# A new hand-over list for a linear-attention-plus-FFT-convolution kernel: order, engines and PSUM banks

## The chip, the cores and the metric

The kernel runs on one core of one Trainium2 chip. The core has engines that each take their own instructions strictly in the order in which the program gives them: TensorE (PE in the profile; its weight loads are shown apart as PEld), VectorE (DVE), ScalarE (ACT), GpSimd (POOL) and SyncE (SP), which here only issues transfers. They wait for one another through semaphores. PE writes its results to eight PSUM banks; DVE and ACT read them, POOL works on SBUF alone. The metric is device microseconds (us) for one execution; lower is better. A difference under about 2% is called no change.

## What is computed

The input is r, k, v, w of shape 4 x 8 x 768 x 48 (batch, heads, time, head width) and u. First comes a recurrence over time for every batch and head, then, on its output seen as 4 x 768 x 384, a gated convolution through the Fourier transform, and an output product:

```python
for t in range(S):
    cur = np.einsum('bhd,bhe->bhde', u[None] * kt, vt)
    y[:, :, t] = np.einsum('bhd,bhde->bhe', rt, state + cur)
    state = wt[:, :, :, None] * state + np.einsum('bhd,bhe->bhde', kt, vt)
...
proj = x @ w_proj
x1, x2, x3 = (proj[..., :D], proj[..., D:2 * D], proj[..., 2 * D:])
x2_conv = np.fft.irfft(np.fft.rfft(x2, n=S, axis=1) * np.fft.rfft(filter_fft, n=S, axis=0), n=S, axis=1)
return ((x1 * x2_conv * x3) @ w_out)
```

## The kernel before

**The two halves of the work.** The 768 time steps of a batch are cut into three groups of 256, so there are twelve groups, numbered 0 to 11 in the names; a group holds two chunks of 128 rows. For each group the kernel loads w, k, r, v (`lw`, `lk`, `lr`, `lv`), takes the logarithm of w on ACT (`ln`), sums it over time on PE (`cs`, lines 1325 and 1328), takes the exponential on ACT (`ex`, `ph`), multiplies k and r with it on DVE (`km`, `qm`, line 1353, tile kq), turns the result round on PE (`tk`, `tq`, line 1366) and copies it out of PSUM (`ck`, `cq`, tile qk). `sc` (line 1464) are the scores, `mt` their masked copy on DVE, `kv` and `ki` the state's product, `su` its scaling on DVE (tile S), `ys`, `yy` and `yi` (lines 1445, 1486, 1500) the output, `xn` its copy, `yt` and `xT` its turned copy. Beside that run small products on plain SBUF tiles: `rk` = r times k, `kw` and `rw` (k and r times w, tile kr), `vb` (v in bf16), `vc` (v times the bonus of u, which comes by `rp`, `rt`, `cp`, `cc`), and `ws`, a product of two rows of w before the logarithm (tile wp). Where `ws` is left out, `ln` takes both rows and `cs` takes twice as many matmuls.

After every third group a batch is complete and its second half can be done: `p` and `q` (line 1712) are two of the projections and `xw` (line 1736) the third, `f` (line 1564) the forward transform, `u` and `z` the product in the frequency domain, `E` (line 1803) the inverse transform, `cE`, `aE`, `dE`, `yE` its putting together and gating, `o` (line 1884) the output product, `co` its copy and `so`, `to` the stores. `cp` and `cq` with two numbers behind them (`cp0.2.0`, `cq0.0.0`) are the copies and gates of the projections; where an `xq` stands ahead of a `cq`, ACT copies the product out of PSUM first and the gate reads SBUF, otherwise the gate reads PSUM. The inverse transform has two forms: folded (`Q`), whose matmuls are shorter and which needs the four `dE` additions behind it, and whole (`P`), which does not.

**Who sets the order.** Nothing is scheduled by a planner when the program is built. A table of text, `ORDER`, has a line for each of some 900 operations: its name, a letter for the engine or form (P PE, A ACT, D DVE, G POOL, S SP; N and B are second forms of DVE and ACT, `-` leaves the operation out), and the PSUM banks of the results that it opens. The program walks the table from top to bottom and issues each operation on the engine named:

```python
o = self.ops.pop(name)
place["how " + name] = e
for key in o.banks:
    place[key] = int(more.pop(0))
if e == NONE:
    continue
got = o.fns[e](e, place)
...
if more and got is not None and more[0] in last:
    tie(got, last[more[0]])
```

So the table sets three things at once: the order on each engine (and on the queue of transfers of SP), the engine of each operation, and the banks. A name at the end of a line (`kw0 G rw0`) is a tie: this operation also waits for that one of DVE. A line `warm 22 2` issues matmuls of zeros on PE into a bank that is free (here 22 units of 256 columns, as 11 matmuls of 512); they compute nothing. All loads and stores but three are issued by SP; `turn` operations with the letter S are transposing transfers, which then need neither PE nor a copy.

Of the kernel before, what the change touches and what calls it, by code (L numbers as in the profile page):

```python
# [89 lines left out]
ph0 A  # L90
# [2 lines left out]
lv1 S
lk2 S
lx1 -
lr2 S
is A
if0 A
sin1 A
um P 4  # L100
warm 4 6
rp0 P 5
rw0 D
qm0 D
kw0 G rw0
rk1 G
vb0 G
warm 8 7
# [63 lines left out]
cq1 A
table A
sc1.0 P 4
lr4 S
rt2 A
dW2 S
dW0 S
lw4 S
ma0.1 -  # L180
mt0.1 D
yy0 P 2
yi0 P
lk4 S
ma1.0 -
lx3 -
xn0 A
xn1 A
rw3 G
vb3 G  # L190
vb2 G
mt1.0 D
ys2 P 6
ys3 P 4
sc1.1 P 2
warm 4 1
cp2 P 0
ma1.1 -
cc2 A
ln2 B  # L200
mt1.1 D
warm 3 1
rp3 P 1
ki3 P 0
kv3 P
cs2 P 2
rt3 A
ln3 B
su3 D
# [152 lines left out]
xq0.0.0 A
sd0.0.0 D
sd0.1.0 D
xq0.2.1 -
rt6 A
f0.0 P 6
cq0.2.1 D
cq0.0.0 N
cc5 D  # L370
cp6 P 4
ws6 G cq0.0.0
lr7 S
lw7 S
lk7 S
lv6 S
cxw1.0 A
cf0.0 A
cc6 D
ys8 P 0  # L380
ys9 P 2
ln6 A
sc4.1 P 4
ma4.1 -
mt4.1 D
kw6 G
rw6 G
f0.1 P 6
lw8 S
lk8 S  # L390
lr8 S
cf0.1 A
cs6 P 4
lx5 -
# [1601 lines left out]
```

## Time and profile before

| what | us |
|---|---|
| median of 3 runs | 151.16 |
| the runs | 149.73, 151.16, 151.60 |
| span of the profiled execution | 149.4 |

The page gives the span of the profiled execution and no time of its own beside it; the lowest of the three runs is 0.3 us above that span. How to read the page: a share of busy time is a share of the span, so PE's 93% says only that some matmul was in flight, since matmuls overlap. More telling is the busy time of each engine in a stretch, and the chain of work that ended last, which is followed backwards from the last instruction to whatever released each step. "A x12" in a row means twelve instructions of one kind in a row. Line numbers are those of the kernel before; in the changed kernel every line is two lower, as its table is two lines shorter.

### The profile page before, as it was taken

Reading aid. Unit: us, or ns where it says so; the run is one execution under the profiler, and the core shown is the slowest. Engines: PE = TensorE matmul, PEld = TensorE weight load, DVE = VectorE, ACT = ScalarE, POOL = GpSimd, SP = SyncE. Lnnn points to the kernel's source line nnn. Section 1 sums busy time; section 2 is a strip of 40 time slices with the busy share of each in tenths; the row PEclk is TensorE's granted clock in tenths of the full one; section 3 lists DMA queues with packets and bytes.
Section 4 is the critical chain, followed back from the end, with each engine's and each line's share of the span. In section 5 each row is a group of like instructions: output and inputs, shape, how many; then the busy total and the mean of one; then the engine's idle time right before and its main releaser. Section 6 shows DMA issues by size and latency. Waiting matters only on the chain.

```text
span 149.4 us, 5795 instructions
## 1 busy us (share of the span) xinstructions
PE 138.7 (93%) x2441; PEld 91.1 (61%) x2441; DVE 123.6 (83%) x239; ACT 120.2 (80%) x200; POOL 91.8 (61%) x104
## 2 busy tenths in 40 slices
PE   7999999999998999999999799999999999999960
PEld 2456766857676766766767555566766566566510
DVE  6999972994859689889999957999987999999920
ACT  3789979869897978899999578898868677687660
POOL 7959979999997439649929676960675006005100
PEclk9999999999999999999999999999999999999995
DMA  4999989999999989999999837799921420502775
GB/s 111 325 321 312 276 193 323 324 257 276 276 251 227 214 214 307 243 281 215 303 202 314 226 59 125 147 275 153 213 103 31 136 53 0 211 24 88 316 254 167
DMA packets 69596, 31.18 MB, mean 209 GB/s; under 512 B 65217, under 2 KB 67778, under 8 KB 69570
## 3 DMA queue, kind: packets, MB, share of 16 engines
q1 hardware_dynamic: 69408, 30.61, 82.9%
q8 instruction: 19, 0.31, 0.8%
q10 hardware_dynamic: 162, 0.20, 0.6%
q14 instruction: 7, 0.06, 0.1%
HBM read 22.41 MB, written 4.72 MB: 182 GB/s over the span
## 4 chain that ended last, share of the span: by engine, by line
PE 60%; POOL 17%; DVE 9%; DMA 5%; issue 3%; ACT 3%; POOLq 0%; SPq 0%; DVEq 0%
PE banks L1712 15%; PE banks L1564 10%; PE banks L1884 8%; PE banks L1736 6%; PE banks L1803 5%; POOL kr L1126 5%; DMA kr<-in_r_dram 5%; POOL rk L1126 4%; POOL vc L1126 4%; PE banks L1486 3%; PE banks L1425 2%; PE banks L1464 2%; DVE kq L1353 2%; PE banks L1366 2%; ACT X L1130 2%
## 5 line engine op out<-in xcount | busy, mean ns | idle before, releaser
L1126 DVE TENSOR_TENSOR mt<-banks,causal 128x1024 bf16<-128x1024 f32 x21 | 25.6, 1220 | 6.6 <-PE banks L1464 6.5
L1712 PE MATMUL banks<-xT,wproj 128*128 128x384 bf16 x144 | 27.1, 326 | 0.5 <-ACT X L1130 0.3
L1353 DVE TENSOR_TENSOR kq<-banks,kr 128x768 bf16<-128x768 f32 x24 | 22.1, 950 | 2.9 <-ACT banks L1336 1.6
L1126 POOL TENSOR_TENSOR rk<-kr 128x768 bf16<-128x768 f32 x11 | 20.0, 1814 | 6.0 <-DVE U L1126 3.2
L1126 POOL TENSOR_TENSOR kr<-kr,w 128x384 f32<-128x384 f32 x21 | 20.6, 998 | 4.9 <-DVE sd L1748 2.8
L1130 ACT ACTIVATE x<-banks 128x768 bf16<-128x768 f32 (+1 forms) x28 | 19.4, 715 | 4.3 <-PE banks L1712 2.3
L1712 PEld LDWEIGHTS <-wproj 128*128 128x128 bf16 x144 | 13.3, 97 | 9.3 <-issue 0.8
L1126 POOL TENSOR_TENSOR vc<-vb,cc 128x768 bf16<-128x768 bf16 x12 | 17.6, 1474 | 1.1 <-DVE mt L1126 0.8
L1126 POOL TENSOR_TENSOR g<-g,x 128x384 bf16<-128x384 bf16 (+1 forms) x5 | 6.0, 1204 | 15.8 <-DVE g L1126 9.4
L1130 ACT ACTIVATE X<-banks 128x768 bf16<-128x768 f32 x12 | 9.8, 814 | 5.4 <-PE banks L1564 4.2
L1564 PE MATMUL banks<-sd,F 128*128 128x384 bf16 (+1 forms) x96 | 13.6, 327 | 0.4 <-ACT X L1130 0.3
L1736 PE MATMUL banks<-wproj,xT 128*128 128x384 bf16 x72 | 13.3, 326 | 0.2 <-ACT wproj L1130 0.2
L1884 PE MATMUL banks<-wout,y 128*128 128x384 bf16 (+1 forms) x78 | 13.5, 328 | 0.1
L1152 PE MATMUL banks<-wt 128*128 128x512 bf16 (+1 forms) x37 | 12.3, 441 | 1.1 <-DVE wt L1219 1.1
L1564 PEld LDWEIGHTS <-F 128*128 128x128 bf16 (+1 forms) x120 | 9.0, 103 | 5.3 <-issue 1.1
L1126 DVE TENSOR_TENSOR U<-X,hh 128x768 bf16<-128x768 bf16 (+1 forms) x17 | 12.1, 728 | 0.2
L1130 ACT ACTIVATE o<-banks 128x768 f32<-128x768 f32 (+1 forms) x13 | 9.6, 768 | 2.9 <-PE banks L1884 2.6
L1130 ACT ACTIVATE xn<-banks 128x384 bf16<-128x384 f32 x24 | 10.6, 491 | 1.2 <-PE banks L1500 1.1
L1464 PE MATMUL banks<-qk 48*64 48x128 bf16 x384 | 10.1, 219 | 0.7 <-DVE kq L1353 0.6
L1130 ACT ACTIVATE qk<-banks 128x1024 bf16<-128x1024 bf16 x10 | 9.9, 1019 | 1.1 <-PE banks L1366 1.1
L1336 ACT ACTIVATE banks<-banks 128x768 f32<-128x768 f32 x12 | 9.6, 799 | 1.0 <-PE banks L1328 0.9
L1126 POOL TENSOR_TENSOR wp<-w 128x384 f32<-128x384 f32 x7 | 7.0, 1005 | 5.1 <-DMA w<-in_w_dram 2.9
(123 smaller groups left out, 312.1 us busy)
## 6 DMA issues: line engine op xcount, KB each, us to landing
w<-in_w_dram SPq DMA_DIRECT2D x12, 384.0 KB, 6.0
kr<-in_k_dram SPq DMA_DIRECT2D x12, 384.0 KB, 5.5
kr<-in_r_dram SPq DMA_DIRECT2D x12, 384.0 KB, 6.0
v<-in_v_dram SPq DMA_DIRECT2D x12, 384.0 KB, 4.8
out_dram<-o SPq DMA_DIRECT2D x11, 384.0 KB, 2.6
o<-in_moe_w_proj_dram SPq DMA_DIRECT2D x4, 384.0 KB, 6.0
U<-in_moe_filter_fft_dram SPq DMA_DIRECT2D x4, 288.0 KB, 8.2
o<-in_moe_w_out_dram SPq DMA_DIRECT2D x1, 384.0 KB
```

Of the source, the lines that this page charges most:

```text
L1126: return eng(e).tensor_mul(o, a, b)
L1130: return nc.scalar.activation(out=o, in_=a, func=AF.Copy)
L1152: nc.tensor.matmul(banks[:, at, lo:hi], wt[:, 0:L], x, start=True, stop=True)
L1336: return nc.scalar.activation(out=p, in_=p, func=AF.Exp)
L1353: op(f"{t}{gi}", [DVE], lambda e, bk, m=m: nc.vector.tensor_mul(kqq[:, m, :, :, 0:D], _mid(two(bk, f"cs{gi}")[:, 1 - m, 0:C].rearrange("p ...
L1464: nc.tensor.matmul(p[spans[c], par, i, jk, :].rearrange("p (j t) -> p j t", j=2), qkk[x, 0, jk, 2 * a + i, spans[c]], qkk[x, 1, :, 2 * a + ...
L1486: nc.tensor.matmul(yview(bk, c)[:, par, hp, :], mt[sm][spans[c], a, par, q, jk, :], vbb[spans[c], 2 * hp + par, jk, :], start=(pi == 0 and ...
L1564: nc.tensor.matmul(p[rows], F[:, ti, c0 + rows.start:c0 + rows.stop], x[q][:, ti, :], start=(ti == 0), stop=(ti == NT - 1),)
L1712: nc.tensor.matmul(o, wproj[:, cb, col0:col0 + L], x, start=(cb == 0), stop=(cb == CB - 1))
L1736: nc.tensor.matmul(view(bk)[:, z], xT[bx][:, c0 + z, cb], wproj[:, cb, C:2 * C], start=(cb == 0), stop=(cb == CB - 1),)
L1803: nc.tensor.matmul(o, P[:, q, m, cs], x, start=start, stop=stop)
L1884: nc.tensor.matmul(view(bk)[:, j] if full else view(bk)[spans[j]], y[cb][:, j, p0:p0 + m], wout[:, cb, :], start=(cb == 0), stop=(cb == CB ...
```

## The change

Only the table `ORDER` differs; the functions are the same. All 915 operations are in both tables. The new table stands in a new order throughout, with other banks, and 140 operations have another letter. The first lines show the kind of change:

```diff
 wz D
 uo D
+imaps G
+maps G
+smalls D
+lw0 S
+lk0 S
+lr0 S
+lw1 S
...
-rk0 D
-rw0 D
-vb0 G
+rk0 G
+rw0 G
+vb0 D
...
-ws4 G
+ws4 -
-cE0.2 B
+cE0.2 A
-aE0.2.0 D
+aE0.2.0 N
...
```

By kind, the letters that change are these. From POOL to DVE, 26: `vb0`, `vc0`, `vc3`, `vc6`, `vc8`, `vc9`, `rw3`, `rk4`, `kw4`, `kw6`, `rk11`, `ws9`, `ws10`, two casts of weights (`eW3`, `eW4`), `kz0`, four gates (`cq0.2.0`, `cq1.2.1`, `cq2.2.1`, `cq3.0.1`), three `sd3` and three `dE`. From DVE to POOL, 14: `rk0`, `rw0`, `kw7`, `rw7`, `sd0.0.0`, three `u`, three `dE`, three `yE`. From ACT to DVE: `ck1`, `cq1`, `cq2`, `ck5`, `xn4`, `xn6`, `xn7`, `rt5`, `rt6`, `vb6`, `eV1`, `co3.2`; the other way `ck2`, `ck4`, four `cc`, `cxw3.5`. `vb4` goes from POOL to ACT. `ws4`, `ws5`, `ws7` and `ws8` are left out. Twelve of the thirteen `xq` copies of ACT and two of three `ma` (the same for scores) are left out, so the gates and masks behind them read PSUM. Eleven `cE` copy the whole inverse transform with ACT instead of half of it, so that 22 `aE` read SBUF only. `E1.2` and `E2.0` take the whole form, and their four `dE` go. `yt4`, `yt6`, `tq6` and `rp9` become transposing transfers on SP. The fillers are 71 units instead of 69, put elsewhere.

At the program's start ACT's list reads as follows, first before, then now. u_r is u in bf16 (the operation `ur`), lg the logarithm of w.

```order
L1235 DMA u_f_142<-in_u_dram 1x384
L1232 ACT_TABLE_LOAD
L1314 ACTIVATE lg1_72<-w1_62 128x8x2x48
L1130 ACTIVATE u_r_143<-u_f_142 1x768
L1314 ACTIVATE lg0_71<-w0_61 128x8x2x48
L1336 ACTIVATE banks_146<-banks_146 128x2x384 x2
L1339 ACTIVATE phi1_78<-banks_146 128x8
```

```order
L1233 DMA u_f_142<-in_u_dram 1x384
L1230 ACT_TABLE_LOAD
L1128 ACTIVATE u_r_143<-u_f_142 1x768
L1312 ACTIVATE lg0_71<-w0_61 128x8x2x48
L1337 ACTIVATE phi0_77<-banks_146 128x8
L1312 ACTIVATE lg1_72<-w1_62 128x8x2x48
L1334 ACTIVATE banks_146<-banks_146 128x2x384 x2
```

The cast of u now stands ahead of both logarithms, and one exponential's column (phi) ahead of the second logarithm.

PE's list at the same place, first the kernel before, where its 11 fillers end (nothing stands ahead of them) and the first sum over time begins, then the new one, from the product with u_r through the 11 fillers to the first sum:

```order
L1152 LDWEIGHTS wt_140
L1152 MATMUL banks_146<-wt_140 128x512
L1325 LDWEIGHTS before_135
L1325 MATMUL banks_146<-lg1_72,before_135 128x384
...
L1325 LDWEIGHTS upto_136
L1325 MATMUL banks_146<-lg1_72,upto_136 128x384
```

```order
L1247 LDWEIGHTS u_r_143
L1247 MATMUL banks_146<-wt1_147,u_r_143 128x1
...
L1150 LDWEIGHTS wt_140
L1150 MATMUL banks_146<-wt_140 128x512
...
L1323 LDWEIGHTS before_135
L1323 MATMUL banks_146<-lg0_71,before_135 128x384
```

Before, the fillers were the first thing on PE; now the six small products with u_r are, and the 11 fillers stand between them and the first `cs`.

DVE's list where group 0's last masks and group 2's first steps stand, before and now (S, mt, kq, kr, vc, vb and qk are the tiles named above, cc the bonus, phi the exponential's column):

```order
L1436 TENSOR_TENSOR S3_95<-banks_146,phi1_78 128x192
L1126 TENSOR_TENSOR mt0_90<-banks_146,causal_138 128x1024
L1126 TENSOR_TENSOR mt1_91<-banks_146,causal_138 128x1024 x2
L1436 TENSOR_TENSOR S0_92<-banks_146,phi1_78 128x192
L1353 TENSOR_TENSOR kq0_73<-banks_146,kr2_66 128x16x48 x2
L1131 COPY cc1_84<-banks_146 128x16
L1353 TENSOR_TENSOR kq1_74<-banks_146,kr0_64 128x16x48 x2
```

```order
L1124 TENSOR_TENSOR mt0_90<-banks_146,causal_138 128x1024
L1124 TENSOR_TENSOR vc0_88<-vb0_85,cc0_83 128x768
L1434 TENSOR_TENSOR S3_95<-banks_146,phi1_78 128x192
L1351 TENSOR_TENSOR kq0_73<-banks_146,kr2_66 128x16x48 x2
L1434 TENSOR_TENSOR S0_92<-banks_146,phi1_78 128x192
L1129 COPY qk0_75<-banks_146 128x1024
L1124 TENSOR_TENSOR mt1_91<-banks_146,causal_138 128x1024
L1124 TENSOR_TENSOR kr0_64<-kr0_64,w0_61 128x8x48
L1351 TENSOR_TENSOR kq1_74<-banks_146,kr0_64 128x16x48 x2
```

DVE now takes a product for vc and one for kr, which POOL did, between its own steps; `rk4`, `kw4` and `vc3` follow in the same way a little later.

More of the change, by code (lines that the diff above doesn't have):

```diff
@@ new lines @@
+mf1.1.1 -
+mf2.0.0 -
+mf2.0.1 -
+mf2.1.0 -
+mf2.1.1 -
+lx2 -
+ws2 -
+ma2.0 -
+ma2.1 -
+xq0.0.0 -
+xq0.2.0 -
+xq0.0.1 -
+xq0.2.1 -
+dE0.0.0 -
+dE0.0.1 -
+dE0.1.0 -
+dE0.1.1 -
+dE0.2.0 -
+dE0.2.1 -
+lx3 -
+ws3 -
+ma3.0 -
+ma3.1 -
+lx4 -
+ws4 -
+ma4.0 -
+ma4.1 -
+yt4 - 0
+lx5 -
+ws5 -
+ma5.0 -
+ma5.1 -
+xq1.2.0 -
+xq1.0.1 -
+xq1.2.1 -
+dE1.2.0 -
+dE1.2.1 -
+lx6 -
+tk6 - 0
+tq6 - 0
+ma6.0 -
+ma6.1 -
+yt6 - 0
+lx7 -
+ws7 -
+ma7.0 -
+ma7.1 -
+yt7 - 0
+lx8 -
+ws8 -
+tk8 - 0
+rp8 - 0
+ma8.0 -
+ma8.1 -
@@ L89 @@
+signs D
+lv0 S
+first A
+ur A
+um P 0
+ln0 B
+warm 22 2
+cs0 P 2
+ia1.0 D
+ia1.1 D
+ub D
+ph0 A
+ia2.1 D
+rw0 G
+ln1 B
+warm 15 7
+cs1 P 0
+ang2 D
+lr2 S
+ia0.1 D
+lw2 S
+lk2 S
+ex0 A
+km0 D
+lv1 S
+lk3 S
+qm0 D
+ex1 A
+diag G
+warm 8 7
+rp0 P 4
+lr3 S
+tk0 P 5
+rt0 D
+lw3 S
+warm 1 7
+cp0 P 4
+vb0 D
+rk1 G
+kv0 P 2
+kw1 G
+rw1 G
+tq0 P 3
+rp1 P 6
 ph1 A
[L90 removed]
 trig A
 sin0 A
[L93 to L96, printed above, removed]
[L97 to L108 removed]
@@ L172 @@
[L172 to L209, printed above, removed]
+sin2 A
+dW2 S
+is A
+ck0 D
+causal G
+su0 D
+ki1 P 2
+kv1 P
+dW0 S
+sin1 A
+km1 D
+warm 3 7
+tk1 P 5
+cq0 A
+qm1 D
+rt1 D
+warm 2 7
+tq1 P 0
+ck1 D
+cc0 A
+rk2 G
+kw2 G
+table A
+ln2 B
+cq1 D
@@ new lines @@
+vb1 G
+rw2 G
+su1 D
+warm 3 7
+sc0.0 P 5
+mt0.0 D
+if3 A
+warm 1 7
+sc1.0 P 0
+mt1.0 D
+lv2 S
+ys1 P 3
+warm 7 7
+sc0.1 P 5
+mt0.1 D
+rp2 P 2
+warm 2 7
+cs2 P 0
+rt2 A
+ex2 A
+vc0 D
+ki2 P 2
+kv2 P
+ph2 A
+dW1 S
+if2 A
+lv3 S
+rk3 G vc0
+su2 D
+yy0 P 5
+yi0 P
+xn0 A
+qm2 D
+km2 D
+ki3 P 2
+xn1 A
+kv3 P
+su3 D
+cp1 P 5
+cc1 A
+lw4 S
+lr4 S
+ln3 B
+tq2 P 6
+if0 A
+ys2 P 4
+if1 A
+ys3 P 0
+cq2 D
+kw3 G
+vc1 G
+sc1.1 P 2
+mt1.1 D
+rw3 D
+eW2 A
+warm 1 7
+cs3 P 6
+ex3 A
+qm3 D
+ph3 A
+km3 D
+tk2 P 2
@@ L360 @@
-rp6 P 4
-xw1.0 P 2
[L362 to L394, printed above, removed]
+xn4 D
+sc3.0 P 6
+mt3.0 D
+xw0.2 P 0
+rk4 D
+xn5 A
+ln4 B
+yt2 P 2
+cp3 P 3
+ys7 P 4
+sc3.1 P 6
+mt3.1 D
+dW3 S
+rw4 G rk4
+cxw0.2 A
+cc3 A
+xT2 A
+kw4 D
+lv4 S
+vc3 D
+cs4 P 0
+ph4 A
+lr6 S
@@ new lines @@
+ex4 A
+xw0.4 P 2
+km4 D
+qm4 D
+p0.0.0 P 6
+lw6 S
+cxw0.4 A
+cp0.0.0 A
+xw0.0 P 2
+rp4 P 6
+ln5 B
+rt4 D
+eW4 D
+ki7 P 7
+yy3 P 0
+yi3 P
+lk6 S
+filt1.0 S
+rk5 G vc3
+xn7 D
+kw5 G
+kv7 P
+su7 D
+tq4 P 6
+filt1.1 S
+cxw0.0 A
+rw5 G
+xn6 D
+cs5 P 2
+tk4 P 7
+sd0.1.0 D
+cq4 A
+ex5 A
+eW3 D
+filt0.1 S
+sd0.0.0 G sd0.1.0
+rp5 P 6
+ph5 A
+cp4 P 0
+cc4 A
+ck4 A
+qm5 D
+rt5 D
+f0.2 P 4
+vb4 A
+filt0.0 S
+km5 D
+lv5 S
+q0.0.0 P 0
+ki8 P 6
+vc4 G
+cq0.0.0 D
+tq5 P 7
+cf0.2 A
+cq5 A
+sc4.0 P 2
+kv8 P
+f0.1 P 4
@@ new lines @@
+kv14 P
+su14 D
+cp1.2.0 A
+ys13 P 4
+cc7 A
+sc6.1 P 0
+mt6.1 D
+q1.2.0 P 6
+cq1.2.0 D
+ws9 D
+ki15 P 7
+lv9 S
+cxw1.4 A
+z0.2 D
+sd1.0.0 D
+p1.0.0 P 2
+cp1.0.0 A
+yy6 P 0
+sd1.1.0 D
+yi6 P
+kv15 P
+ln9 A
+rt8 S
+su15 D
+sc7.0 P 2
+tq8 P 6
+xn13 A
+kw9 G sd1.1.0
+ck8 S
+lv8 S
+rw9 G sd1.1.0
+xn12 A
+cq8 A
+vc7 G
+cs9 P 4
+lk10 S
+mt7.0 D
+p1.0.1 P 0
+lw10 S
+lw11 S
+f1.0 P 6
+ex9 A
+ph9 A
+km9 D
+f1.2 P 2
+qm9 D
+xT6 S
+cp1.0.1 A
+z0.0 D
+q1.0.0 P 0
+cf1.0 A
+ys14 P 4
+ys15 P 6
+cf1.2 A
+u01.2 G z0.0
```

1236 lines of the change are left out of this document (505 added, 731 removed).

## The prediction

> **What bounds the kernel now.** I read the busy time of each engine by stage first, since the page's shares are means over stages, then the chain of work that ended last, then the start and the end as timelines, and last the groups of instructions, for prices. Engines by stage (start and end, length, busy us and instructions of each, granted clock, share of the DMA engines, GB/s):
>
> ```profile
> 20.00:45.00 25.00, 24.33 (x566) 17.79 (x563) 17.09 (x24) 21.69 (x39) 24.46 (x23) 1.00 1.02 280
> 45.00:143.80 98.80, 95.71 (x1611) 62.49 (x1610) 89.09 (x155) 81.34 (x140) 51.42 (x43) 1.00 0.79 180
> ```
>
> The order in a row is PE, PEld, DVE, ACT, POOL. From 20 to 45 us POOL is busy 24.46 of 25 us and DVE only 17.09. From 45 us on PE is busy 95.71 of 98.8 us and DVE 89.09. So there are two bounds: POOL to about 45 us, then PE, with DVE close behind. The chain that ended last says the same: from the landing of one r to a kq pair of DVE (start, length, what), all that it has between these two rows is POOL's, but for pauses of 1.8 us in all.
>
> ```profile
> 13.20 6.83 DMA kr<-in_r_dram
> ...
> 44.95 0.97 DVE kq L1353
> ```
>
> At 45.92 the last `qm5` of this chain is done, and from there PE's own instructions are most of the chain. I take 45.9 as the seam between the stages.
>
> **The start.** Here are the first table load, the two logarithms with u's cast between them, PE's 11 fillers and first sum, the first kq pair and the first mt, and the packets of the queue that only u and the last stores use, between 1.5 and 2 us:
>
> ```profile
> 1.35 1.28 ACT L1232 ACT_TABLE_LOAD   x1 [1.35 <-PEq L1980]
> 4.33 0.84 ACT L1314 ACTIVATE lg<-w 128x768 bf16<-128x768 f32 x1 [1.69 <-DMA w<-in_w_dram]
> 5.08 0.83 ACT L1130 ACTIVATE u_r<-u_f 1x768 bf16<-1x768 f32 x1
> 7.15 0.80 ACT L1336 ACTIVATE banks<-banks 128x768 f32<-128x768 f32 x1 [0.51 <-PE banks L1328]
> ...
> 1.12 4.87 PE L1152 MATMUL banks<-wt 128*128 128x512 bf16 x11 [1.12 <-DVE wt L1219]
> 5.78 0.82 PE L1325 MATMUL banks<-lg,before 128*128 128x384 bf16 x2
> ...
> 9.69 1.97 DVE L1353 TENSOR_TENSOR kq<-banks,kr 128x768 bf16<-128x768 f32 x2
> 16.39 1.21 DVE L1126 TENSOR_TENSOR mt<-banks,causal 128x1024 bf16<-128x1024 f32 x1
> ...
> q10 hardware_dynamic: 2, 0.00, 1.2%
> ```
>
> The new table puts u's cast first on ACT and its product first on PE. u has landed soon after 2 us, so the cast runs from 2.63 (1.35 + 1.28) to 3.46, and PE begins with it instead of at 1.12. The six small products take some 0.3, so the 11 fillers run from about 3.8 and, at the 4.87 of the row, to 8.6. The first sum took from 5.78 to 7.15 less the wait, 1.3 us: done at 9.9. Then phi (0.2), the second logarithm (0.84) and the exponential (0.80) stand in line on ACT: 11.7. The kq pair runs from 11.7 to 13.7, where it ended at 11.66: 2.0 us later. POOL, which now makes group 0's rk and kr itself, is no later: r and k of group 0 had landed when DVE started its rk, and 1.81 and twice 1.00 behind that end near 11.9.
>
> **The first stage.** Prices (busy, mean ns, idle before it):
>
> ```profile
> L1126 DVE TENSOR_TENSOR mt<-banks,causal 128x1024 bf16<-128x1024 f32 x21 | 25.6, 1220 | 6.6 <-PE banks L1464 6.5
> L1353 DVE TENSOR_TENSOR kq<-banks,kr 128x768 bf16<-128x768 f32 x24 | 22.1, 950 | 2.9 <-ACT banks L1336 1.6 <-POOL kr L1126 0.7 <-issue 0.2
> L1126 POOL TENSOR_TENSOR rk<-kr 128x768 bf16<-128x768 f32 x11 | 20.0, 1814 | 6.0 <-DVE U L1126 3.2 <-DVE P L1776 1.4 <-PE banks L1486 1.1
> L1126 POOL TENSOR_TENSOR vc<-vb,cc 128x768 bf16<-128x768 bf16 x12 | 17.6, 1474 | 1.1 <-DVE mt L1126 0.8
> L1126 POOL TENSOR_TENSOR wp<-w 128x384 f32<-128x384 f32 x7 | 7.0, 1005 | 5.1 <-DMA w<-in_w_dram 2.9 <-DVE U L1126 2.2
> L1436 DVE TENSOR_TENSOR S<-banks,phi 128x192 bf16<-128x192 f32 x20 | 6.9, 351 | 2.2 <-PE banks L1425 2.0
> L1131 DVE COPY qk<-banks 128x1024 bf16<-128x1024 bf16 x6 | 4.1, 681 | 1.1 <-PE banks L1366 1.1
> L1126 DVE TENSOR_TENSOR rk<-kr 128x768 bf16<-128x768 f32 x1 | 1.0, 959 | 0.0
> L1131 DVE COPY rt<-banks 128x768 bf16<-128x768 bf16 x3 | 1.7, 554 | 0.7 <-ACT x L1130 0.7
> L1748 DVE TENSOR_TENSOR sd<-x 128x1152 bf16<-128x1152 bf16 x6 | 4.4, 762 | 0.0
> ```
>
> POOL loses `vc0`, `vc3` (2 x 1.47), `rk4` (1.81), `rw3`, `kw4`, `ws4`, `ws5` (4 x 1.0): 8.8 us, and four casts, against 2.8 for `rk0` and `rw0` at the start. So POOL ceases to bind. DVE is next: after the kq pair come a PSUM copy of 0.55, a cast (no DVE row for it; between 0.35 and 0.95, taken as 0.6), 0.68, 0.35, a kq pair, 0.55, two qk copies, 0.35 and the first mt: 8.0 less 0.06 for each of eleven, since two kq in a row took 1.82 to 1.97 and not always 1.90, so 7.3. The first mt is done at 21.0, against 17.6 before.
>
> From there to the end of group 5's kq pair the new table has on DVE seven mt (8.5), eight kq (7.6), five S (1.8), two qk (1.4), two copies of 0.55, three `xn` (1.6), one sd (0.8), two casts (0.9) and the five products taken from POOL: `rk4` 0.96, `rw3` and `kw4` 0.56 each, `vc0` and `vc3`, which DVE never did before and which lie between 0.55 (a bf16 product of that size) and 0.96; I take 0.95, as one operand is f32. Together 27.7, less 0.06 x 35: 25.6. So this stage ends at 46.6 if DVE never waits, against 45.9: **+0.7**. Its ends: -1.5, if the casts, the vc and the fillers come at their lower ends; +5, if the next paragraph's wait falls on every product. What PE has behind it there is the same work in both tables, group 5's turned tiles next.
>
> Two DVE rows and one of POOL show that wait: a DVE product of two SBUF tiles that meets a POOL operation.
>
> ```profile
> L1126 DVE TENSOR_TENSOR kr<-kr,w x3: 541/558/1202, 9.0 to 62.8; 128x384 f32<-128x384 f32 x3
> ...
> 61.39 1.20 DVE L1126 TENSOR_TENSOR kr<-kr,w 128x384 f32<-128x384 f32 x1
> ...
> 61.27 0.90 POOL L1126 TENSOR_TENSOR g<-g,x 128x384 bf16<-128x384 bf16 x1
> ```
>
> One of three kr products took 1.20 instead of 0.55: it began at 61.39 while POOL ran until 62.17, and ended 0.42 after that. In the stage before 45.9 the old table has such DVE products only at its start; the new one has six, and most have a tie that holds back the POOL operation behind them, not the one ahead.
>
> [...]
>
> **The second stage, bound by PE.** Prices from the chain (the whole and the folded inverse transform, turned tiles, sums), then what in it is not PE's:
>
> ```profile
> 46.38 0.55 PE banks L1366 x8
> 57.04 0.34 PE banks L1525 x6
> 59.56 0.82 ACT X L1130
> 84.58 0.99 issue
> 87.17 0.82 ACT X L1130
> 92.07 1.00 PE banks L1803 x6
> 95.08 0.50 PE banks L1325 x2
> 105.00 0.66 PE banks L1803 x6
> 110.03 0.82 ACT X L1130
> 114.20 0.82 ACT o L1130
> ```
>
> Behind the seam PE loses the four turned tiles that become transfers (0.55 + 3 x 0.34 = 1.57), gains two whole inverse transforms for folded ones (2 x 0.34), and two sums that take both rows of w (0.4 to 0.5 each, from the 0.50 that two 384-column matmuls last when nothing follows): **0.0**. Six filler units stand late (0.2 us for each 512 columns, 0.6 in all); they fill waits, and cost 0.6 if there is none. The four transfers go to SP's queue, where loads stand behind them; the eight qk transfers of before landed in a median of 4.8 us, and nothing on PE waited for one.
>
> ACT's two copies that change most, one per gate and one per inverse transform:
>
> ```profile
> L1130 ACT ACTIVATE g<-banks 128x768 bf16<-128x768 f32 x7 | 5.6, 816 | 0.1
> L1823 ACT ACTIVATE ev<-banks 128x384 f32<-128x384 f32 x12 | 5.8, 494 | 1.1 <-PE banks L1803 1.1
> ```
>
> ACT loses twelve copies `xq`, six of 0.82 and six of half that width, which is 7.9 at the 0.50 of a 384-wide copy, and gains 0.82 - 0.49 for each of eleven `cE`, 3.6; with the two `ma` and the turned copies that go it gets some 7 us lighter of 81. On DVE the sums that read SBUF instead of PSUM and the `dE`, `yE` and `u` that go make up, within 1 us over the list, for the gates that now read PSUM and the products from POOL. Four pieces of the chain are ACT's, 0.82 each, and one is 0.99 of issue: 4.3 us that PE does not hide. A lighter ACT queue takes away the part in which ACT was late, not the copy itself. I take **-1.3**; the ends are -4.3 (all of them gone) and +3 (gates that hold their banks until DVE, 89.09 of 98.8 us busy, reads them, which costs PE waits of its own).
>
> **The end.** The last pieces of the chain:
>
> ```profile
> 143.85 0.65 ACT o L1130
> 144.56 0.48 ACT o L1130
> ```
>
> Two copies on ACT stand one behind the other after PE's last product. The new table gives the last one to DVE, and the wide one starts two products earlier. That takes between 0 and 0.65 from the end: **-0.3**.
>
> **Sum.** 149.4 + 0.7 + 0.0 - 1.3 - 0.3 = 148.5 for a span. The lowest run lies 0.3 above the profiled span and the median of the runs 1.8 above it; read as a median, 148.5 + 1.8 = 150.3.
>
> **Rivals.** First, faster: the stages overlap better than the sum grants, so that all 4.3 us in the chain that are not PE's go (3.0 more than I took) and the first stage ends 1.5 early instead of 0.7 late (2.2 more): 150.3 - 5.2 = 145.1. For it: ACT gets 7 us lighter, POOL at least 8.8 in the stage it bound. Against it: DVE takes over in that stage, and the start is 2.0 later.
>
> Second, slower, DVE blocked by POOL: the six products of the first stage and the two or three casts beside them each wait about 0.65 (1.20 less 0.55), some 5.5 us, and then PE, which has no spare time after the seam, ends that much later: 150.3 + 5.5 - 0.7 = 155.1. For it: the 1.20 row, and a POOL that is still busy most of that stage. Against it: the ties, and only one of three such products in the old trace was long. It decides once DVE loses more than about 4 us there.
>
> Third, that it does nothing: total PE work is the same within 1 us and PE's 95.71 of 98.8 cannot shrink. This is near my forecast and gives 151.
>
> **How the numbers follow.** No change beyond 2% (which is about what a measurement of this kernel can tell; 3.0 us, so 148.1 to 154.2) is the likeliest at 0.46: the forecast and the third rival. Faster gets 0.32, since one and a half of its two gains are enough to pass 148.1. Slower gets 0.22, the second rival or late PSUM banks. The likeliest case alone reaches from 148.1 to 153. For 8 in 10 the range goes to the first rival's time and nearly to the second's: 145.1 to 154.8.
>
> **What would show it.** Right: PE's first filler near 3.8 us and the first kq pair near 11.7; POOL's busy time from 20 to 45 us well under 20 of 25 and DVE's above 22; group 5's kq pair done near 46.6; PE busy over 96% from there to its end; the last copy on DVE. Wrong: DVE products of kr, rk or vc with a maximum above 1.1 us, or PE waits on DVE in the second stage (slower); a kq pair of group 5 before 44 us, or PE without pieces of ACT in the chain (faster).

## The result, and the profile after

The changed kernel is slower: the ratio of its runs to those of the kernel before is 1.040, with a 95% interval of 1.029 to 1.050. The runs of before in the same session took 149.59 to 151.60 us (median 150.44), those of the changed kernel 155.57, 156.85, 158.55 and 158.59; runs more than 1.5% above the fastest of the same kernel, as the last two, stay out of every ratio here and below. The profiled execution is the one of 155.57 us, with a span of 153.9 against 149.4. A second set of runs of the same changed kernel, later, gave 1.034 [1.024, 1.044].

The page's totals for the changed kernel, engine by engine, and the shares of the chain that ended last:

```profile
PE 138.6 (90%) x2441; PEld 91.3 (59%) x2441; DVE 134.6 (87%) x250; ACT 111.3 (72%) x180; POOL 79.2 (51%) x87
...
PE 67%; DVE 14%; ACT 8%; issue 4%; DMA 4%; ACTq 0%; SPq 0%; DVEq 0%
```

PE was busy 138.7 us of 149.4 before and is busy 138.6 of 153.9 now. So all of the 4.5 us is time in which PE stands still: 10.7 us before, 15.3 now. POOL's 17% of the old chain is gone from it, DVE's share has gone from 9 to 14%. Where PE stands still, the busy times by stretch tell (length, then busy us and instructions of PE, PEld, DVE, ACT and POOL, granted clock, share of the DMA engines, GB/s). First the kernel before:

```profile
0.00:20.00 20.00, 18.05 (x271) 10.62 (x274) 17.46 (x62) 15.98 (x21) 15.91 (x39) 1.00 0.96 258
...
45.00:85.00 40.00, 38.43 (x805) 26.87 (x803) 36.33 (x50) 35.75 (x63) 26.63 (x23) 1.00 1.16 255
85.00:115.00 30.00, 28.61 (x578) 18.56 (x578) 25.54 (x43) 24.39 (x44) 19.54 (x16) 1.00 0.72 138
115.00:149.40 34.40, 29.29 (x232) 17.24 (x231) 27.22 (x64) 22.39 (x37) 5.25 (x5) 0.96 0.39 136
```

and the changed kernel:

```profile
0.00:20.00 20.00, 15.13 (x192) 9.08 (x193) 18.03 (x60) 12.69 (x16) 17.13 (x39) 1.00 1.03 280
20.00:45.00 25.00, 23.58 (x597) 17.50 (x596) 23.14 (x32) 21.52 (x38) 14.51 (x13) 1.00 0.99 277
45.00:85.00 40.00, 38.70 (x752) 26.04 (x750) 36.93 (x51) 32.41 (x59) 26.70 (x20) 1.00 1.05 224
85.00:115.00 30.00, 27.01 (x576) 17.54 (x578) 26.31 (x42) 21.19 (x37) 14.08 (x11) 1.00 0.99 174
115.00:153.90 38.90, 34.21 (x338) 21.09 (x334) 30.22 (x70) 23.50 (x35) 6.77 (x6) 0.97 0.41 137
```

Length less PE's busy time is PE's idle time:

| stretch | before | changed | more |
|---|---|---|---|
| 0 to 20 us | 1.95 | 4.87 | 2.92 |
| 20 to 45 us | 0.67 | 1.42 | 0.75 |
| 45 to 85 us | 1.57 | 1.30 | -0.27 |
| 85 to 115 us | 1.39 | 2.99 | 1.60 |
| 115 us to the end | 5.11 | 4.69 | -0.42 |

The rows cut through one pause of the kernel before: 0.42 of the 0.99 us from 84.58 on (the `issue` row of the prediction) fall ahead of 85 us. So 45 to 115 us is better read as one: 2.96 before, 4.29 now, 1.33 more, and nothing is gained up to 85 us.

Two stretches carry the loss: the start, and 85 to 115 us. The start of the changed kernel as a timeline (PE's product with u_r, fillers and first sum; ACT's phi, second logarithm and exponential; POOL; DVE):

```profile
3.54 0.32 PE L1247 MATMUL banks<-wt,u_r 1*128 1x1 bf16 x6 [3.54 <-ACT u_r L1128]
3.78 4.69 PE L1150 MATMUL banks<-wt 128*128 128x512 bf16 x11
8.31 0.49 PE L1323 MATMUL banks<-lg,before 128*128 128x384 bf16 x2
...
10.15 0.80 ACT L1334 ACTIVATE banks<-banks 128x768 f32<-128x768 f32 x1
...
8.72 2.30 POOL L1124 TENSOR_TENSOR kr<-kr,w 128x384 f32<-128x384 f32 x2
...
6.89 1.87 DVE L1589 TENSOR_SCALAR U<-o,fcol 128x192 int32<-128x192 f32 x1
9.01 1.16 DVE L1550 TENSOR_SCALAR o<-o,tcol 128x384 int32<-128x384 f32 x1
10.27 0.87 DVE L1589 TENSOR_SCALAR U<-o,fcol 128x192 int32<-128x192 f32 x1
11.35 1.82 DVE L1351 TENSOR_TENSOR kq<-banks,kr 128x768 bf16<-128x768 f32 x2
19.36 3.49 DVE L1124 TENSOR_TENSOR mt<-banks,causal 128x1024 bf16<-128x1024 f32 x3 [0.23 <-PE banks L1462]
```

PE begins at 3.54 instead of 1.12. The first kq pair begins at 11.35 instead of 9.69, and three chains arrive there together: the exponential at 10.95, POOL's kr at 11.02, DVE's own index operations at 11.4. These index operations took 0.3 to 0.45 us elsewhere in the start and up to 1.87 beside POOL's products. Group 5's kq pair, the seam of the prediction, on DVE:

```profile
42.84 0.99 DVE L1129 CAST wproj<-o 128x384 bf16<-128x384 f32 x1
...
46.08 0.95 DVE L1351 TENSOR_TENSOR kq<-banks,kr 128x768 bf16<-128x768 f32 x1
...
47.41 0.95 DVE L1351 TENSOR_TENSOR kq<-banks,kr 128x768 bf16<-128x768 f32 x1
```

It ends at 48.36. From the first mt's end (20.58) to there DVE is busy 25.92 of 27.78 us and waits 1.86, by the profile nearly all of it for PE: 1.2 us in three waits for scores (L1462), 0.6 in one for an output (L1498). The chain that ended last agrees. From 24.75 to 47.9 us all of it is PE's, but for two masks of DVE and pauses of 1.0 us in all:

```profile
27.24 1.24 DVE mt L1124
...
33.10 1.24 DVE mt L1124
```

In the kernel before, the same stretch of the chain was POOL's (the prediction's first section). So PE itself, started late, is what the changed kernel's first stage follows. Behind the seam, three places where PE waits, with ACT's queue between them (61.5 us; 88 us; 107 to 110 us):

```profile
61.48 1.35 DVE L1129 CAST vb<-v 128x768 bf16<-128x768 f32 x1
62.88 0.43 PE L1423 MATMUL banks<-vb,kq 64*64 64x48 bf16 x16 [0.66 <-DVE vb L1129]
...
89.39 0.82 PE L1801 MATMUL banks<-mi,P 128*128 128x384 bf16 x4 [1.45 <-issue]
...
107.57 0.85 ACT L1128 ACTIVATE vb<-v 128x768 bf16<-128x768 f32 x1 [1.09 <-DMA v<-in_v_dram]
108.33 1.49 ACT L1128 ACTIVATE o<-banks 128x768 f32<-128x768 f32 x2
109.17 0.24 PE L1429 MATMUL banks<-S,ident 128*128 128x192 bf16 x1 [0.38 <-ACT o L1128]
109.87 0.57 PE L1484 MATMUL banks<-vb,mt 64*128 64x48 bf16 x32 [0.46 <-ACT o L1128]
```

The last load of v lands at 107.55; ACT's cast waits for it, two copies of outputs stand behind the cast in ACT's queue, and PE waits for the banks that these copies free. The profile names ACT's o, but the transfer is what was late. In both lists two weight loads and a turning transfer stand right ahead of this load; SP reached it at 96.73 us before and at 101.54 now, as it stood still until 95.42 for the transfer of group 8's outputs. No wait of PE that the profile lists for the changed kernel ends on a transfer, and none on a gate of DVE.

### The profile page after: what moved, and what is told of

It is laid out like the page before. It is cut to its first block, busy times and chain, and to the rows that moved or that the text cites. A ratio compares the mean times of both kernels' runs of the same rounds, so it can differ in the third digit from the quotient of the medians.

```text
span 153.9 us, 5771 instructions
## 1 busy us (share of the span) xinstructions
PE 138.6 (90%) x2441; PEld 91.3 (59%) x2441; DVE 134.6 (87%) x250; ACT 111.3 (72%) x180; POOL 79.2 (51%) x87
## 4 chain that ended last, share of the span: by engine, by line
PE 67%; DVE 14%; ACT 8%; issue 4%; DMA 4%; ACTq 0%; SPq 0%; DVEq 0%
PE banks L1710 12%; PE banks L1562 7%; PE banks L1734 6%; PE banks L1882 6%; PE banks L1801 6%; DVE mt L1124 6%; PE banks L1150 5%; DMA v<-in_v_dram 4%; PE banks L1462 4%; PE banks L1323 4%; PE banks L1364 3%; PE banks L1484 3%; PE banks L1423 2%; PE banks L1443 2%; PE banks L1498 2%
## 5 line engine op out<-in xcount | busy, mean ns | idle before, releaser
L1124 DVE TENSOR_TENSOR mt<-banks,causal 128x1024 bf16<-128x1024 f32 x23 | 27.9, 1222 | 2.1 <-PE banks L1462 1.4
L1124 POOL TENSOR_TENSOR kr<-kr,w 128x384 f32<-128x384 f32 x21 | 21.6, 1045 | 12.8 <-DVE rk L1124 8.7
L1710 PE MATMUL banks<-xT,wproj 128*128 128x384 bf16 x144 | 28.0, 326 | 0.3 <-ACT g L1128 0.3
L1124 POOL TENSOR_TENSOR rk<-kr 128x768 bf16<-128x768 f32 x10 | 18.2, 1820 | 8.9 <-DVE vc L1124 5.3
L1124 POOL TENSOR_TENSOR y<-y,g 128x768 bf16<-128x768 bf16 (+1 forms) x4 | 5.8, 1458 | 16.1 <-DVE P L1774 10.6
L1562 PE MATMUL banks<-sd,F 128*128 128x384 bf16 (+1 forms) x96 | 13.8, 328 | 0.3
L1124 POOL TENSOR_TENSOR vc<-vb,cc 128x768 bf16<-128x768 bf16 x7 | 10.3, 1475 | 6.8 <-DVE P L1774 3.3
L1124 DVE TENSOR_TENSOR g<-banks,x 128x384 bf16<-128x384 f32 (+1 forms) x15 | 10.9, 739 | 3.2 <-ACT x L1128 2.6
L1128 ACT ACTIVATE ev<-banks 128x768 bf16<-128x768 f32 x11 | 8.7, 812 | 6.3 <-PE banks L1801 4.4
L1462 PE MATMUL banks<-qk 48*64 48x128 bf16 x384 | 10.8, 219 | 1.3 <-issue 0.8
L1128 ACT ACTIVATE xn<-banks 128x384 bf16<-128x384 f32 x21 | 9.2, 488 | 3.0 <-PE banks L1498 2.9
L1124 POOL TENSOR_TENSOR U<-X,hh 128x768 bf16<-128x768 bf16 x4 | 6.5, 1644 | 8.0 <-DVE U L1124 7.0
```

Of the source, the lines that this page charges most:

```text
L1124: return eng(e).tensor_mul(o, a, b)
L1128: return nc.scalar.activation(out=o, in_=a, func=AF.Copy)
L1462: nc.tensor.matmul(p[spans[c], par, i, jk, :].rearrange("p (j t) -> p j t", j=2), qkk[x, 0, jk, 2 * a + i, spans[c]], qkk[x, 1, :, 2 * a + ...
L1562: nc.tensor.matmul(p[rows], F[:, ti, c0 + rows.start:c0 + rows.stop], x[q][:, ti, :], start=(ti == 0), stop=(ti == NT - 1),)
L1710: nc.tensor.matmul(o, wproj[:, cb, col0:col0 + L], x, start=(cb == 0), stop=(cb == CB - 1))
```

## The experiments

Ratios are to the kernel before, with their 95% intervals; the changed kernel itself stands at 1.040 and 1.034. "Idle" is PE's idle time as above.

**Parts of the two lists put together.** In these four kernels one list runs up to a named PE operation, and then follow the rows of the other that are left, in their own order. A few banks are renumbered where two results would meet.

head16_before: the old list up to `sc0.0` (the first 16 us), then the new one (edit against the changed kernel).

```diff
-imaps G
-maps G
...
-um P 0
...
-sc0.0 P 5
+fills D
+smalls D
...
+um P 4
...
+sc0.0 P 6
```

> The rows of the old list up to the scores sc0.0 of group 0 (the first 16 us), then the rows of the new list that are left, in their order. In the changed kernel the first mt is done 3.0 us later than before. Theory A (late start: what is lost there is never made up, because DVE and then PE have no spare time behind it): about 2 us come back, some 153.5 us against the changed kernel's 155.6. Rival B (the start is hidden behind later waits of DVE, the loss lies in the list behind it): 155 to 156, no change. Rival C (casts and products of DVE that wait for POOL in the first stage make the loss): 155 to 156 too, the long DVE operations stay.

Measured 1.034 [1.028, 1.040]: no gain. But the two lists do not join well here. One filler unit waited for a bank that a mask still read, and PE lost as much in the first 20 us as in the changed kernel:

```profile
19.09 0.27 PE L1151 MATMUL banks<-wt 128*128 128x256 bf16 x1 [2.18 <-DVE mt L1125]
```

So this run says nothing about what the early start is worth in the new list.

head16_after: the reverse (edit against the kernel before).

```diff
-fills D
...
-um P 4
...
+imaps G
...
+um P 0
...
+sc0.0 P 5
```

> The reverse: the new list up to sc0.0, then what is left of the old one. Theory A: the old kernel gets some 2 us slower, 152 to 153 against 150.4. Rival B: no change, 150 to 151, since POOL binds the old first stage and starts no later.

Measured 1.025 [1.018, 1.032]: slower than the kernel before, though the interval does not clear the 2% that counts as a change. Its first three rows by stretch:

```profile
0.00:20.00 20.00, 15.09 (x182) 9.03 (x183) 18.11 (x60) 12.85 (x17) 17.20 (x39) 1.00 1.03 283
20.00:45.00 25.00, 23.98 (x587) 17.26 (x587) 17.39 (x23) 19.43 (x37) 22.17 (x20) 0.93 0.84 241
45.00:85.00 40.00, 38.94 (x743) 27.72 (x743) 34.60 (x49) 36.80 (x65) 27.56 (x25) 1.00 1.11 237
```

PE's idle time in the first 20 us is 4.91, as in the changed kernel, and its span is 152.5, 3.1 more than before. Over the whole span PE stands still 13.4 us, 2.7 more than before; this execution also has a stretch at a lower granted clock (0.82 from 22 to 30 us, 0.93 over 20 to 45). The new start alone costs the old kernel 2.5%, and nothing behind it makes that up.

head44_before and head85_before: the old list up to `kv8` (44 us) and up to `yi7` (84 us), then the new one (the edit is the second's, against the changed kernel).

```diff
+fills D
...
+kv8 P
...
-lv10 S
...
```

> The old list up to kv8 (the first 44 us, the whole first stage), then what is left of the new one. If all is lost in the start and the first stage: 150 to 151. Theory A with a second loss of some 2.5 us behind the seam (a cast of v at 61 us, the last load of v at 108 us): 153 to 153.5, as with the first 16 us. Rival D (the new list's second stage is bound by DVE, 92.9 of 104 us busy, so it takes as long whenever it begins): 155 or more.

> The old list up to yi7 (some 84 us), then what is left of the new one, with the last loads of v behind the turning transfers. If the late load at 108 us costs what PE waits there, 1.1 us: 151.5. If the new list's last third is no worse, because the old list loses as much there in other places: 150 to 150.5. If DVE's ten us in the chain from 118 to 128 us are a bound of their own: 153 or more.

Measured 1.035 [1.027, 1.042] and 1.026 [1.019, 1.034]. Both are slower than the old kernel by most of the whole difference, though the start is the old one. Part of it is made at the joint: PE waited 1.4 us for sd in the one and 1.3 us for mt in the other, at the places where the lists meet. Start alone 2.5%, last part alone at most 2.6%, both together 3.4 to 4.0%. Without the 1.3 us at its joint the last part would be some 1.7%, by estimate; with intervals this wide (head85_before does not clear 2% either) these runs can't tell whether the parts add up.

**The start.** fillers_first puts the fillers ahead of u's product again, and the second logarithm ahead of phi:

```diff
+ln0 B
 ur A
-um P 0
-ln0 B
 warm 22 2
 cs0 P 2
+um P 6
...
+ln1 B
 ph0 A
...
-ln1 B
```

> In the changed kernel PE's 11 fillers stand ahead of u's product again, u's cast behind the first logarithm, the second logarithm ahead of phi. Nothing else. If the order on PE and ACT alone makes the late start: group 0's kq pair begins near 9.7 instead of 11.35 us and the time falls by 1.5 to 2 us from 155.6 to 156.9. Rival (DVE and POOL are as late: DVE is busy until 11.35 with index operations that took 1.87, 1.16 and 0.87 us beside POOL's products of r, k and w, and POOL's last kr ends at 11.02): kq pair at 11.0 to 11.4, gain 0.3 us or less.

Measured 1.045 [1.040, 1.049]: the rival's case, and rather slower (all five runs had a granted clock of only 0.971 to 0.988). The kq pair began at 11.32. POOL's products and DVE's index operations are where they were:

```profile
6.90 1.85 DVE L1589 TENSOR_SCALAR U<-o,fcol 128x192 int32<-128x192 f32 x1
...
11.32 1.80 DVE L1351 TENSOR_TENSOR kq<-banks,kr 128x768 bf16<-128x768 f32 x2
...
11.31 0.50 PE L1381 MATMUL banks<-ident,rk 128*128 128x128 bf16 x6 [0.62 <-POOL ident L1140]
```

PE was ready earlier and then waited. old_start_ops is this kernel and also puts group 0's rk and rw back on DVE:

```diff
-rk0 G
-kw0 G
...
-rw0 G
+rk0 D
+kw0 G
+rw0 D
 km0 D
```

> The same, and group 0's rk and the product of r with w back on DVE, right ahead of the kq pair, as in the kernel before. If POOL's products slow DVE's index operations down: these are back to 0.3 to 0.45 us each, the kq pair begins at 9.7 to 10.2, the first mt is done near 18 instead of 20.6, and 1 to 2 us of the time come back (154 to 155.5). Rival (DVE binds the first stage, 1.5 us more work on it eats what is gained; or ACT's sines ahead of cq0 set the first scores at 18.8 anyway): no gain.

Measured 1.034 [1.028, 1.041]: no gain. Its DVE rows (in the profiled execution, of 163.94 us, PE's granted clock was 0.85; the ratio rests on two runs of 155.48 and 154.71):

```profile
7.33 0.32 DVE L1589 TENSOR_SCALAR U<-o,fcol 128x192 int32<-128x192 f32 x1
...
7.89 0.42 DVE L1550 TENSOR_SCALAR o<-o,tcol 128x384 int32<-128x384 f32 x1
...
8.41 0.31 DVE L1589 TENSOR_SCALAR U<-o,fcol 128x192 int32<-128x192 f32 x1
...
11.35 1.82 DVE L1351 TENSOR_TENSOR kq<-banks,kr 128x768 bf16<-128x768 f32 x2 [0.89 <-POOL kr L1124]
```

With POOL at rest beside them the three index operations took 0.32, 0.42 and 0.31 instead of 1.87, 1.16 and 0.87: that half of the theory is shown. But POOL's kr, now behind DVE's rk, ends at 11.32, and the kq pair begins at 11.35 again. Two of the three chains had been shortened (ACT's exponential ended at 9.83), and the third held.

**Single waits of the second stage.** vb6_on_act:

```diff
+vb6 A
 hc1 A
...
-vb6 D
```

> In the changed kernel the cast of group 6's v stands on ACT ahead of a pair of filter copies instead of on DVE, where it took 1.35 us beside a POOL product and PE waited for it at 62.2 us. If that wait reaches the end: 0.7 to 0.8 us less. Rival (the old list put it on ACT too, and copies of the filter behind it then come late, h2 or hg1 hold PE instead): no gain.

Measured 1.037 [1.032, 1.042]: no gain that can be told. The wait for vb is gone; in the profiled execution PE then lost it to a stretch at half clock (0.50 from 88.40 to 91.80 us; last section). That is not the whole reason: two other runs had a granted clock of 1.000 and took 155.67 and 154.68 us, as the changed kernel does.

last_v_early:

```diff
 lv10 S
+lv11 S
...
-lv11 S
```

> In the changed kernel the last load of v is issued right behind the one ahead of it, no longer behind two weight loads and the turning transfer of group 11. If its landing at 107.6 us is what PE waits for: the chain loses its piece of 6.01 us of DMA, the waits of PE between 107.7 and 110 us (0.6 + 0.6) go, 1.0 to 1.2 us less. Rival (DVE's unbroken work from 117.9 to 128.4 us in the chain is the next bound): gain under 0.4 us.

Measured 1.035 [1.029, 1.042]. The wait moved: w_out's loads now stand behind this one, ACT waits for them, a score copy waits behind that on ACT, and PE for the copy.

```profile
104.84 0.84 ACT L1128 ACTIVATE wout<-o 128x768 bf16<-128x768 f32 x1 [1.02 <-DMA o<-in_moe_w_out_dram]
105.59 1.00 ACT L1128 ACTIVATE mt<-banks 128x1024 bf16<-128x1024 f32 x1
...
PE banks L1882 <- ACT mt L1128: 1.1, 1, 1.1
```

loads_early puts all four loads ahead of group 8's turning transfer:

```diff
+lv10 S
+dV0 S
+dV1 S
+lv11 S
 xT8 S
```

> In the changed kernel the last two loads of v and the two of w_out are issued ahead of the transposing transfers that SP reached at 95.4 us, so at about 92 us. Moving the last load of v alone did not help: PE then waited 1.2 us for w_out's loads, which it had been put ahead of. If late loads behind transposing transfers are what PE waits for between 104 and 110 us: both waits go, 1.0 to 1.2 us less than the changed kernel's 155.6 to 156.9. Rival (DVE, 89% busy from 45 us on, is the bound and the waits only show where it surfaces): less than 0.4 us.

Measured 1.050 [1.044, 1.055], higher still, though the intervals overlap: PE now waits for that transfer.

```profile
PE banks L1734 <- DMA xT<-xn: 2.7, 1, 2.7
```

loads_behind_rt9 finds a place ahead of SP's long pause:

```diff
 rt9 S
+lv11 S
+lv10 S
...
```

> In the changed kernel the last two loads of v are issued behind group 9's turning transfer, at some 86 us, where both buffers are free and SP then waits until 95.4 for group 8's outputs; nothing is put ahead of a transfer that PE waits for. If the late load is a loss of its own: PE's waits at 107.7 to 110 us go and 1.0 to 1.2 us with them. Rival (DVE binds the second stage): no gain.

Measured 1.041 [1.033, 1.048]. PE's waits behind ACT's o are gone, its idle time from 85 to 115 us is 2.52 instead of 2.99, and the time is the same within the interval.

dve_relief:

```diff
-vc0 D
+vc0 G
...
-rk3 G vc0
+rk3 G
...
-rk4 D
+rk4 G
...
-vc3 D
+vc3 G
```

> In the changed kernel vc0, vc3 and rk4 go back from DVE (0.95 us each) to POOL, and the three ties that hold a POOL product behind them go. If DVE binds the new first stage (busy 35.8 of 38 us from 8 to 46 us): group 5's kq pair is done 1.5 to 2.8 us ahead of 48.4, and the time falls by 1.5 to 2 us. Rival 1 (PE's work and waits behind it decide, the first stage's lateness is made up there): under 0.5 us. Rival 2 (POOL becomes the bound again): slower.

Measured 1.037 [1.031, 1.043]. DVE is lighter and the pair no earlier (its second half begins at 47.96 instead of 47.41). Part of that is a later start in this execution, whose first mt began at 20.12 instead of 19.36, as PE's first sums took 1.24 us instead of 0.65; from there on some 0.2 us is gained:

```profile
20.00:45.00 25.00, 23.66 (x620) 17.32 (x619) 21.26 (x27) 21.82 (x37) 19.19 (x16) 1.00 0.94 264
...
47.96 0.94 DVE L1351 TENSOR_TENSOR kq<-banks,kr 128x768 bf16<-128x768 f32 x1
```

So DVE's 23.14 of 25 us was not what set the end of that stage, as the chain above says.

**Several at once.** second_stage has the loads of loads_early, vb6 on ACT, `E0.2` ahead of `kv18`, and neither `warm 4 0` nor `warm 2 5`; both_stages adds dve_relief.

```diff
-warm 4 0
-warm 2 5
+E0.2 P 4
 kv18 P 3
 kv16 P
 sc8.0 P 0
-E0.2 P 4
```

> Four local losses of the new second stage are taken out of the changed kernel together: the loads as above, the cast of group 6's v on ACT, the folded inverse transform E0.2 ahead of kv18 and kv16 instead of behind them (PE stood still for 1.45 us in the midst of it, behind 88 short products in a row, without a wait that the profile shows), and the six late filler units. If these are separate losses of PE: 1.1 + 0.8 + 0.5 to 1.4 + 0.6, so 3 to 3.9 us less, 152 to 153. Rival (they hide one another, or DVE is the bound): under 1.5 us.

> The second and the third of these kernels in one. If first stage and second stage each lose on their own: the sum of their gains, some 5 us, 150 to 151, as fast as the kernel before. If the second stage eats what the first gives back: no more than the better of the two.

The runs of second_stage took 155.32, 157.70, 160.66 and 161.59 us, so there is no ratio; both_stages measured 1.040 [1.036, 1.044]. In both, PE waited 2.3 us for group 8's transfer, as in loads_early, and DVE's relief added nothing. local_losses_out is second_stage with the loads behind rt9; sums_narrow also has `ws4` and `ws5` on POOL.

```diff
-ws4 -
+ws4 G
...
-ln4 B
+ln4 A
```

> The changed kernel itself, unchanged, beside the three others: 155.5 to 157, and its full clock granted from 6.4 to 9.7 us on, as in the runs of it and of its variants so far (4.9 to 7.1 where the fillers come first).

> These loads, with the cast of group 6's v on ACT, E0.2 ahead of kv18 and kv16, and without the six late filler units. In the run that had these last three, PE stood 1.6 us ahead of the changed kernel at 94 us, of which 0.8 came from the start, and lost it to group 8's turning transfer. If the losses add up: 1.1 + 0.8 + 0.4 + 0.4, so 2 to 2.7 us less, 153 to 154. Rival (DVE): at most 1 us.

> The same, and the products ws4 and ws5 of groups 4 and 5 back on POOL, so that their sums take 6 products instead of 12, and their logarithms 384 columns. If PE bounds from 30 us on: 2 x 0.4 to 0.5 us of PE less, 0.8 to 1.0 us on top of the kernel above. Rival (POOL's two products of 1.0 us delay its own kr and rk, or PE waits there anyway): under 0.3 us.

changed_again, with no edit, is the 1.034 named above. local_losses_out measured 1.031 [1.019, 1.043], the lowest ratio of the variants of the changed kernel, but from two runs (153.39 and 155.43) and not apart from the changed kernel's; its profiled span is 151.7 with an idle time of 13.8 against 15.0 to 15.3. About 1 us of the forecast 2 to 2.7 is the most that these rows support. sums_narrow measured 1.047 [1.039, 1.055], slower. Here POOL's `ws5` (38.66 to 39.66 us) runs beside a kr product of DVE, which takes 1.40 us instead of 0.55 and ends 0.42 behind POOL, as in the 1.20 row of the prediction; PE waits 0.9 us for the kq pair behind it:

```profile
38.68 1.40 DVE L1122 TENSOR_TENSOR kr<-kr,w 128x384 f32<-128x384 f32 x1
```

**One part alone, one part undone.** old_transfers is the kernel before with the change's four turning transfers only:

```diff
-yt4 P 6
+yt4 - 0
...
-xT4 D
+xT4 S
...
-tq6 P 5
+tq6 - 0
...
-cq6 D
+cq6 S
...
```

> The kernel before with one part of the change alone: the four tiles that PE turned and an engine copied back (tq6, yt4, yt6, rp9) become turning transfers on SP's queue. If PE bounds and nothing waits for them: PE loses 0.55 + 3 x 0.34 us, so 1.0 to 1.6 us less than 149.7 to 150. If loads and later transfers on SP come late by them, or PE waits for the turned tile itself (4.8 us from issue to landing): as slow or slower, up to 2 us.

Measured 1.026 [1.023, 1.030]. PE has 26 matmuls less to do, 1.6 us by the prediction's prices, and the kernel takes 3.9 us more. PE's waits for transfers in its profiled execution (157.06 us, the six others 152.85 to 154.13, so that the waits were as long in those is not shown):

```profile
PE banks L1397 <- DMA rt<-rk: 2.3, 1, 2.3
PE banks L1464 <- DMA qk<-kq: 0.9, 1, 0.9
```

gates_copied undoes the gates in the changed kernel:

```diff
-cq0.0.0 D
+xq0.0.0 A
+cq0.0.0 N
...
```

> The changed kernel with another part undone alone: ACT copies the gates out of PSUM again (six of 0.82 and six of 0.50 us) and DVE multiplies two SBUF tiles instead. If gates that read PSUM are a gain, as forecast: 1 to 1.5 us slower than the changed kernel's 154.2 to 156.9. Rival (DVE's queue is what the second stage waits for; it gets 3.7 us lighter): 1 us or more faster. If neither engine is the bound there: within 0.7 us.

Measured 1.092 [1.086, 1.097], some 8 us more than the changed kernel. The copies stand in an ACT queue whose order was not made for them, so this is no price of the copies, and it does not show by itself that the gates cost nothing. What speaks for that is the list of PE's waits in the changed kernel, where none ends on a gate of DVE.

## Why the prediction was wrong, point by point

**Total work: right.** "0.0" for PE's work came out as 138.7 against 138.6 us busy. With that the whole question was where PE would stand still, and the prediction did not ask it in this form. Behind the seam, for which the 0.0 was meant, it is 0.79 us more, since 0.98 us of fillers stand there and none did before.

**The start: right in its numbers, wrong in its cause and its price.** Fillers at 3.8 and their end were met (3.78 and 8.5), the kq pair was forecast from 11.7 to 13.7 and ran from 11.35 to 13.17, the first mt was forecast done at 21.0 and was at 20.6. (The terms listed for that add up to 7.6, not 8.0; less 0.7 they give 20.6.) As the cause it named PE and ACT's queue alone. It put POOL's end near 11.9, behind its own 11.7, and still called POOL "no later", and DVE's index operations are not in it; POOL (11.02) and DVE (11.4) were just as late, and fillers_first and old_start_ops show that taking one or two of the three away gives nothing.

**The first stage, +0.7: this step failed.** It took DVE's operations from the first mt to the seam, 25.6 us "if DVE never waits", and set the rest aside with "What PE has behind it there is the same work in both tables". The sum was right: DVE was busy 25.92 us. The condition was not: DVE waited 1.86 us, nearly all of it for PE, and the seam came at 48.36, 2.4 later than before instead of 0.7. dve_relief agrees that DVE was not what set the end: 1.9 us less of it moved the stage forward by some 0.2. What PE had lost by then was its own idle time, 2.92 in the first 20 us and 0.75 more to 45 us, and head16_after shows that the new start alone, with the old list behind it, goes through to the end at 2.5%. The step read "POOL binds" in the old profile as if PE had time to spare there; its 24.33 of 25 us stood in the same row.

**The second stage, -1.3: this step failed too, in sign, and by more.** From the seam to the end the kernel before took 103.5 us and the changed one 105.5: 2.1 more, where 0.0 - 1.3 - 0.3 was forecast. 0.79 of it is PE's work (above), 1.27 its idle time. The step's premise came true: ACT got lighter (120.2 to 111.3 us; 7 was forecast). But PE's waits did not get fewer by it. From 45 to 115 us they grew by 1.33 us: the pause behind 1631 matmuls took 1.45 instead of 0.99, and two waits of 0.38 and 0.46 behind the last load of v, which SP reached 4.8 us later, are new. The prediction noted that loads stand behind the four new transfers and gave them no price because nothing on PE had waited for the eight of before. In the changed kernel's profile PE waits for none of the four either. old_transfers shows what they cost in the old list, where their places were not made for them: 2.6%, with less work for PE. That they cost as much in the new list was not tried. The feared cause of loss, gates that hold their banks until DVE reads them, is in no wait of PE that the profile lists.

**The end, -0.3: right**, 0.42 less idle time from 115 us on.

**The second rival** (DVE blocked by POOL, 155.1) had nearly the time, but not the cause. The products that it named were not long: kr 0.55, rk and vc 0.95 each. In the first stage POOL was at rest beside them, held by the ties that the prediction counted against this rival; where a POOL product does run beside one, it is long (1.40 instead of 0.55 in sums_narrow). Index operations and casts did meet POOL's products, and were long: 1.87, 1.16 and 0.87 us for three index operations that took 0.32, 0.42 and 0.31 with POOL at rest, 2.9 us more in all, and casts of 1.04 and 1.35 us (128x768) and 0.99 us (128x384), where a 128x768 cast begun 0.16 us ahead of POOL's product took 0.55 and a 128x384 cast with POOL at rest 0.34. But undoing it for the index operations changed no time.

**What stays open.** Of the 4.5 us, 2.9 arise in the first 20 us, 0.75 up to 45 and 1.3 from 45 to 115 us, and 0.4 is gained at the end; that is read from the profile. That the new start makes the old kernel slower by itself is shown, at 2.5%. For the last part it is not: head85_before has 1.3 us of its own at the joint. That taking out the local waits of the second stage gives back more than about 1 us is not shown either. No variant came near the kernel before.

## What to carry to other kernels

Where the bound engine has the same work before and after, the time is that work plus its idle time: make the forecast as a list of where it will stand still, from the first microsecond, and treat a later first instruction as a loss until a named slack takes it up. A tuned order has several chains that arrive together, so shortening one shows nothing: here two of three chains shortened at the start, and each wait of the second stage alone, gave back no time that could be told. A turned tile moved from PE to a transfer is not free because PE loses work: in old_transfers PE waited 2.3 and 0.9 us for two such tiles. And a forecast "if this engine never waits" needs a look at the engine that it would wait for.
